# Attention and a spectral filter on one core: the first four scores ahead of the branch, three loads moved

## Chip, core and metric

The kernel runs on one core of a Trainium2 chip. The metric is the device time of one execution in microseconds, median of several runs. A profiled execution beside them gives the trace from which all rows below are taken.

## What is computed

Two independent blocks on inputs of 2048 rows by 448 columns, joined along the last axis:

```python
# A: 16 heads of 28, one common key and value (float32)
q = (x @ wq).reshape(B, S, H, Dh).transpose(0, 2, 1, 3)
k, v = x @ wk, x @ wv
p = softmax(einsum("bhqd,bkd->bhqk", q, k) * Dh ** -0.5)
a = einsum("bhqk,bkd->bhqd", p, v).transpose(0, 2, 1, 3).reshape(B, S, H * Dh) @ wo
# B: filter in the frequency domain
y = irfft2(rfft2(x) * (w_r + 1j * w_i), s=(S, D))
```

## The kernel before

**Stages.** A first stage projects x to q, k and v (L325), and interleaves with it the first transform of block B, in eight units q = 0 to 7: `fft1_a` (products L139, evicted to `a` at L145), then `fft1_b` (products L158, evicted to `bs` at L166 or L168 by `fft1_out`, and stored to `t1` in DRAM with two DMAs each, L173). Then comes a branch on the data, and behind it 256 steps of attention.

**The branch.** A shift for the softmax (`cvec`) is made from a bound. If the bound is too high (`bits` over a constant, L449), a loop computes exact maxima instead; with the inputs here the path is not taken. Every engine loads the value for itself (L448, TENSOR_LOAD), compares and branches. The branch cannot be interleaved with anything: what stands ahead of it in the program is issued ahead of it on its engine. The taken path writes two of the six PSUM banks `s0` to `s5`, and rebuilds the first q.

Just ahead of the branch stand: copies of the first q's high and low halves (`qh`, `ql`) into `qf`, done by ScalarE (L192), VectorE (L194), SP's and POOL's queues (L195); the products of unit 6 into two banks (`pb6`), the tiny products for `bits` (bank `pb3`, L434), unit 7's two halves (L139; the second one stays in bank `pa7`), and 16 transposes of v into a bank `pv` (L445). Right behind it stand the eviction of `pa7` (ScalarE, L145), those of `pb6` with its two stores, that of `pv` into `vs` (L486), and the second half of the keys `ka`: a cast (L254), a difference (L255) and three copies by SP (L257).

**The steps.** Step number `step` is one block of 128 keys for one group of four heads and 512 queries: four scores (L771, one bank each), four exponentials on ScalarE (L772) that free the banks, and later four products with `vs` (L747) into an output bank. Free banks are handed out by a queue (`take`, `scored`, `give`). PLAN is a list of batches of one to three steps; in a step's string each dash is a score and a letter is a unit of other work: F the last unit of the first transform (`fft1_b(7)`), A and B the halves of the second transform, W the output projection, Z the third transform. A batch's products with `vs` follow at its end. TensorE's order is that of the program; so is VectorE's behind the branch. The other queues are ordered by the library's planner, which places an instruction when its inputs are ready in its own estimate; `behind(x, y)` adds an order of issue and no wait.

**Loads for the transforms.** `at(step, f)` calls f at the end of a step. `fft2_load(0)` is called at step 0: four loads from `t1` by SP (L541) and four of the filter's weights by POOL (L546). They wait for the stores of unit 7. `fft2_split` (L558, L559) prepares the first A unit (L528). `build_q` for the second group stands at step 3: eight copies (L212) and one (L214) by SP.

After the last B unit, VectorE evicts it into `cst`, SP stores it to `t2` (L594), and `fft3_load(0)` reads it back as `c2` in four loads by SP (L609; r is the half, l the quarter in it), with the matrix `fi` loaded by POOL (L611). Their reader is `fft3_a` (L618).

Of the kernel before, what the change touches and what calls it, by code (L numbers as in the profile page):

```python
# [37 lines left out]
def batch(*units):  # L38

    return [("----" + u) if i else ("---" + u + "-") for i, u in enumerate(units)]  # L40


A, B, BACK = [batch(u, "", "") for u in "ABZ"]
CHUNK = 4 * [batch("W", "W", "W")] + 2 * [batch("W", "W", "")]
ONE, PAIR = batch(""), batch("", "")
PLAN = ([batch("F"), ONE] + 4 * [PAIR] + [batch("A", ""), A] + 10 * [B, A] + CHUNK + 4 * [B, A] + [B, B, ONE]
        + 5 * [BACK] + CHUNK + 14 * [BACK] + CHUNK + 13 * [BACK])

ROOM = {"A": 0, "B": 2, "W": 2, "Z": 1, "": 1, "F": 0}
# [7 lines left out]
def kernel(ctx: ExitStack, tc: tile.TileContext, t: dict):  # L57
    nc = tc.nc
    mm = nc.tensor.matmul
# [12 lines left out]
    ka = cp.tile([128, S], F32R, name="ka")  # L72
# [6 lines left out]
    def behind(ins, other):  # L79

        tc.add_manual_dep(ins.ins, other.ins.name,
                          mybir.DependencyInfo(mybir.DependencyClass.NoSync, mybir.DependencyReason.DATA),
                          reason="order of issue")
# [59 lines left out]
    def fft1_a_out(q, p, pa):  # L143
        a = at1[q, p] = fp.tile([128, 2, DF], F32, name="a", tag=("pwr", "pwi")[p])
        return nc.scalar.activation(a, pa, AF.Copy)  # L145
# [4 lines left out]
    def fft1_mm(q, pb=None):  # L150
        w = xb[q][1]
        if pb is None:
            pb = aux2("pbb"), ps_o.tile([128, 2, DF], F32, name="po")
        for p in range(2):
            a = at1.pop((q, p))
            for h in range(2):
                for e in range(2):
                    mm(pb[h][64 * e:64 * e + 64, p], w[64 * h:64 * h + 64, 2 * p + e], a[64 * h:64 * h + 64, e],  # L158
                       start=True, stop=True)
        return pb  # L160

    def fft1_out(q, pb, after=None):
        bs = fp.tile([128, 2, 2, DF], F32, name="bs", tag=("cst", "cst", "wr", "b2")[q // 2])
        for h in range(2):
            if q < 6:
                ev = nc.scalar.activation(bs[:, h], pb[h], AF.Copy)  # L166
            else:
                ev = nc.vector.tensor_copy(bs[:, h], pb[h])  # L168
                if after is not None:
                    behind(ev, after)  # L170
        for e in range(2):
            n0 = 16 * e + 2 * q
            stored.append(nc.sync.dma_start(t1.rearrange("(l s) n f -> s l n f", l=2)[:, :, n0:n0 + 2],  # L173
                                            bs[64 * e:64 * e + 64]))
        return ev
# [10 lines left out]
    qa = {}  # L186
# [35 lines left out]
    free = deque(ps_s.tile([128, 512], F32, name=f"s{i}") for i in range(BANKS))  # L222

    def bank():
        free.rotate(-1)
        return free[-1]

    def pair_of(b):
        return b[:, :2 * DF].rearrange("p (n f) -> p n f", n=2)


    with tc.tile_pool(name="w1", bufs=1) as w1:
# [37 lines left out]
        with tc.tile_pool(name="x1", bufs=2) as x1:  # L270
# [104 lines left out]
            for c in range(1, NC):  # L375
                for g in range(NG):
# [22 lines left out]
                    n = 4 * (c - 1) + g  # L399
                    if n in slots:  # L400
                        q = slots.index(n)
                        fft1_a(q)
                        fft1_load(q + 4)
                        if n == 10:
# [3 lines left out]
                            qf, qh, ql = build_q(0, 0, True)  # L408
# [22 lines left out]
        pb6 = fft1_mm(6, [pair_of(bank()) for _ in range(2)])  # L431
# [3 lines left out]
        bound = nc.vector.tensor_reduce(bits, pb3[0:1, 0:16], axis=AX.X, op=ALU.max)  # L435
# [7 lines left out]
        pv = bank().rearrange("p (b d) -> p b d", b=16)  # L443
        for b in range(16):
            nc.tensor.transpose(pv[:, b], kf[32:64, b * 128:(b + 1) * 128], ident[32:64, 32:64])  # L445


        rv = nc.values_load(bits.bitcast(I32)[0:1, 0:1])  # L448
        with tc.If(rv > int(np.float32(BOUND).view(np.int32))), tc.tile_pool(name="g1", bufs=1) as g1:  # L449
            k4 = g1.tile([128, S], F32, name="k4")  # L450
            nc.vector.memset(k4, 0.0)
            for i in range(4):
                nc.vector.tensor_copy(k4[32 * i:32 * i + DH], kf[0:DH])
            mz = g1.tile([128, 4, 32], F32, name="mz")
            nc.vector.memset(mz, 0.0)


            qv = qraw.rearrange("p g (b q) -> p (g b) q", q=128)
            banks = free[2], free[3]
            with tc.For_i(0, 64, 1) as n:  # L460
                qs = g1.tile([128, 128], F32, name="qs")
                nc.vector.tensor_copy(qs, qv[:, bass.ds(n, 1)][:, 0])
                mx = g1.tile([128, 4, 4], F32, name="mx")
                for i in range(4):
                    r = slice(32 * i, 32 * i + 32)
                    for h in range(4):
                        ps = banks[0]
                        mm(ps, qs[r], k4[r, h * 512:(h + 1) * 512], start=True, stop=True)
                        nc.vector.tensor_reduce(mx[:, i, h:h + 1], ps, axis=AX.X, op=ALU.max)
                nc.vector.tensor_reduce(mz[:, :, DH], mx, axis=AX.X, op=ALU.max)  # L470
                pt = banks[1][:, :128]
                mm(pt, mz.rearrange("p i d -> p (i d)"), ident, start=True, stop=True)
                nc.vector.scalar_tensor_tensor(qs, qs, mask, pt, op0=ALU.mult, op1=ALU.add)
                nc.vector.tensor_copy(qv[:, bass.ds(n, 1)][:, 0], qs)
            nc.vector.memset(cvec, 0.0)
            nc.vector.memset(mask, 1.0)
            qf, qh, ql = build_q(0, 0, True)
            for i in range(4):
                for p in range(4):
                    on_dve = copy_q(i, p, qf, (qh, ql)[p % 2], nc.vector)  # L480
            on_act = nc.scalar.activation(bits, bits, AF.Copy)


        behind(fft1_a_out(7, 1, pa7), on_act)
        on_dve = fft1_out(6, pb6, on_dve)
        ev = nc.vector.tensor_copy(vs, pv)  # L486
        behind(ev, on_dve)
        on_dve = ev
# [2 lines left out]

    ctx.enter_context(tc.manual_schedule(engines={mybir.EngineType.DVE}))

    d, f, a, b, e, c = free
    free.clear()
    free.extend((a, b, d, e, f, c))
    take, late = free.popleft, []

    def give(bank, scores=1):

        late.append([scores, bank])
# [10 lines left out]
    begun = []  # L512
# [88 lines left out]
    t2v = t2.rearrange("(r l n) h f -> r l h n f", r=2, l=2)  # L601
    c2 = {}

    def fft3_load(q):
        c2["c", q] = fp.tile([128, 4, DF], F32, name="c2", tag="b2")
        for r in range(2):
            for l in range(2):
                p = (r * 2 + l) * 32
                nc.sync.dma_start(c2["c", q][p:p + 32], t2v[r, l][:, 4 * q:4 * q + 4])  # L609
        c2["F", q] = fp.tile([128, 4, 128], F32, name="fi", tag="wr")  # L610
        behind(nc.gpsimd.dma_start(c2["F", q], t["fi"][:, 4 * q:4 * q + 4]), begun[-1])  # L611

# [80 lines left out]
    def at(step, f, *a):  # L693
        later.setdefault(max(step, 0), []).append((f, a))
# [8 lines left out]
    place, where, room = [], {}, []  # L703
    for b, steps in enumerate(PLAN):
        for i, s in enumerate(steps):
# [4 lines left out]
        first = units[:1] == "Z" and (len(where["Z"]) - 1) % 4 < 2  # L710
        room.append(2 if first else ROOM[units[:1]])
    fft2_consts()
    at(0, fft2_load, 0)
    at(where["A"][0] - 1, fft2_split, 0)
    at(14, fft3_consts)
    for u, step in enumerate(where["A"]):
# [10 lines left out]
    for g in range(NC * NG - 1):  # L727
        n = next(n for n in range(16 * g + 3, 16 * g + 13) if place[n][1] < 2 and room[place[n][0]])
# [10 lines left out]
    step = 0  # L739
# [19 lines left out]
    for c, g in order:  # L759
        for kc in range(16):  # L760
            ps, n = [], 0
            b, i = place[step]
            for k in PLAN[b][i]:
                if k != "-":
                    f, *a = todo[k].popleft()
                    f(*a)
                    continue
                if n % 2 == 0:
                    ps.append(pp.tile([128, 2, CW], F32, name="p"))
                sc = take()  # L770
                begun.append(mm(sc, ka[:, kc * 128:(kc + 1) * 128], qa[c, g][:, n], start=True, stop=True))  # L771
                nc.scalar.activation(ps[-1][:, n % 2], sc, AF.Exp, scale=SCALE)  # L772
                scored(sc)
                n += 1
            pend.append((c, g, kc, ps))
            if i + 1 == len(PLAN[b]) and step < 255:
                flush(min(KEEP, len(PLAN[b])))
            if step == 1:
                give(ps_x.tile([128, 512], F32, name="sx", tag="aux"))
                give(ps_o.tile([128, 512], F32, name="po"))  # L780
            for f, a in later.pop(step, []):
                f(*a)
            if step in builds:
                build_q(*order[step // 16 + 1])
            elif norms and i < 2 and room[b] and step > waits_for_output(norms[0][0]):
                room[b] -= 1
                norm(*norms.popleft())
            step += 1
# [3 lines left out]
    c = NC - 1  # L792
# [15 lines left out]
    for k in range(4):  # L808
        p = ws[k]
# [120 lines left out]
```

## Time and profile before

| | us |
|---|---|
| median of 3 runs | 657.26 (657.15 to 657.98) |
| profiled execution | 655.57 |
| its span | 653.8 |
| TensorE busy in the span | 646.0 |
| ScalarE busy | 554.9 |
| VectorE busy | 361.7 |

The profiled execution is one execution, 1.69 us under the median of the three runs; times inside it are counted from the start of the span. The granted clock was 1.00. Busy shares of TensorE overlap by modelled ends of pipelined products, so a share of 99% does not say that it runs at its peak; the wait lists and the times from one row to the next say more. In rows, "idle before <-x" names what ended the engine's idle time, as inferred from the semaphores.

### The profile page before, as it was taken

The page shows a single profiled execution, that of the slowest core. Times are in us where ns is not written, and L with a number is a line of the kernel's source. Part 1 is how long each engine was busy: PE and PEld are TensorE (multiplying, and loading weights), DVE is VectorE, ACT ScalarE, POOL GpSimd, SP SyncE. Part 2 cuts the span into 40 slices and gives each one's busy share as a digit, 9 for nine tenths or more (in the row PEclk, how much of TensorE's full clock was granted, in tenths as well). Part 3 has the DMA queues.
Part 4 walks back from the last instruction along what each step waited for, and adds up shares of the span by engine and source line. Part 5 has one row for each costly group of instructions (what it writes and reads, how often), then busy time and mean ns, then how long its engine had stood idle before and what let it go on. Part 6 is the DMA issues. An engine that isn't in the chain of part 4 may idle for free.

```text
span 653.8 us, 11925 instructions
## 1 busy us (share of the span) xinstructions
PE 646.0 (99%) x4480; PEld 377.3 (58%) x4480; DVE 361.7 (55%) x810; ACT 554.9 (85%) x1100; POOL 59.2 (9%) x109
## 2 busy tenths in 40 slices
PE   9999999999999999999999999999999999999997
PEld 6877554555545566455545655656565565565655
DVE  6999546767788832377763601465533421553533
ACT  5555899999999988899989987999999788999991
POOL 3022301101101100000000000010011000010010
PEclk9999999999999999999999999999999999999999
DMA  8756952525453323121151303123231403240001
GB/s 281 255 174 168 255 149 77 140 69 147 123 144 86 94 70 93 44 61 50 48 147 55 84 29 78 43 77 76 74 79 33 106 29 94 59 110 15 14 29 58
DMA packets 34572, 62.40 MB, mean 95 GB/s; under 512 B 6657, under 2 KB 22930, under 8 KB 33548
## 3 DMA queue, kind: packets, MB, share of 16 engines
q1 hardware_dynamic: 30736, 49.44, 26.8%
q0 software_dynamic: 3200, 11.26, 6.7%
q8 instruction: 36, 0.59, 0.4%
q10 hardware_dynamic: 576, 0.92, 0.4%
q14 instruction: 24, 0.20, 0.1%
HBM read 29.35 MB, written 14.75 MB: 67 GB/s over the span
## 4 chain that ended last, share of the span: by engine, by line
PE 86%; SPq 1%; DMA 1%; DVE 1%; ACT 0%; issue 0%; ACTq 0%; DVEq 0%
PE s L771 29%; PE s L747 28%; PE sx L771 5%; PE po L771 5%; PE po L747 4%; PE s L667 4%; PE sx L747 2%; PE s L630 2%; PE s L618 1%; PE sx L667 1%; PE po L667 1%; SPq L212 1%; PE s L530 1%; PE s L529 1%; PE s L528 1%; PE sx L618 1%
## 5 line engine op out<-in xcount | busy, mean ns | idle before, releaser
L772 ACT ACTIVATE p<-s 128x512 f32<-128x512 f32 x767 | 416.7, 651 | 48.3 <-PE s L771 48.0
L771 PE MATMUL s<-qa,ka 128*128 128x512 f32 x767 | 238.3, 408 | 1.0 <-DVE vs L486 1.0
L747 PE MATMUL s<-p,vs 128*32 128x512 f32 x1664 | 193.8, 596 | 0.0
L771 PEld LDWEIGHTS s<-qa,ka 128*128 128x128 f32 x767 | 138.7, 188 | 88.8 <-ACT p L772 50.7
L747 PEld LDWEIGHTS s<-p,vs 128*32 128x32 f32 x1664 | 46.8, 109 | 105.0 <-issue 100.5
L772 ACT ACTIVATE p<-sx 128x512 f32<-128x512 f32 x133 | 86.3, 649 | 2.5 <-PE sx L771 2.5
L772 ACT ACTIVATE p<-po 128x512 f32<-128x512 f32 x124 | 79.9, 644 | 2.8 <-PE po L771 2.8
L655 DVE RECIPROCAL r<-r 128x128 f32<-128x128 f32 x64 | 61.0, 953 | 2.2
L771 PE MATMUL sx<-qa,ka 128*128 128x512 f32 x133 | 53.1, 399 | 0.0
L771 PE MATMUL po<-qa,ka 128*128 128x512 f32 x124 | 50.3, 405 | 0.0
L638 POOL TENSOR_TENSOR yo<-y 128x226 f32<-128x226 f32 x16 | 10.1, 632 | 292.8 <-issue 252.7
L674 DVE COPY ya<-s 128x448 f32<-128x448 f32 x7 | 4.4, 625 | 56.8 <-PE s L667 56.8
L771 PEld LDWEIGHTS sx<-qa,ka 128*128 128x128 f32 x133 | 25.0, 188 | 10.8 <-ACT p L772 5.9
L747 PE MATMUL po<-p,vs 128*32 128x512 f32 x256 | 29.9, 596 | 0.0
L771 PEld LDWEIGHTS po<-qa,ka 128*128 128x128 f32 x124 | 23.3, 188 | 10.0 <-ACT p L772 6.2
L632 DVE COPY m<-s 128x452 f32<-128x452 f32 x13 | 8.2, 629 | 33.9 <-PE s L630 33.9
L620 DVE COPY z<-s 112x512 f32<-112x512 f32 (+1 forms) x11 | 7.6, 692 | 33.6 <-PE s L618 30.7
L325 PE MATMUL s<-xh,wqh 128*128 128x512 f32 x64 | 25.8, 403 | 0.2 <-ACT wqh L307 0.2
L325 PE MATMUL s<-xh,wql 128*128 128x512 f32 x64 | 25.1, 392 | 0.1
L329 ACT ACTIVATE qraw<-s 128x512 f32<-128x512 f32 x16 | 9.3, 600 | 16.7 <-PE s L325 16.6
L755 DVE COPY osb<-s 128x512 f32<-128x512 f32 x12 | 8.3, 690 | 21.5 <-PE s L747 21.5
L656 DVE TENSOR_TENSOR osb<-osb,r 128x128 f32<-128x128 f32 x64 | 18.7, 292 | 2.2
(188 smaller groups left out, 717.0 us busy)
## 6 DMA issues: line engine op xcount, KB each, us to landing
qa<-qa SPq DMA_DIRECT2D x15, 512.0 KB, 5.4
raw<-xa SPq DMA_DIRECT2D x16, 256.0 KB, 5.0
xb<-xb SPq DMA_DIRECT2D x8, 512.0 KB, 3.5
qa<-qh SPq DMA_DIRECT2D x64, 64.0 KB, 2.0
qa<-ql SPq DMA_DIRECT2D x60, 64.0 KB, 2.0
ob<-yo SPq DMA_DIRECT2D x16, 226.0 KB
t<-bs SPq DMA_DIRECT2D x16, 225.0 KB, 3.4
wr<-wr POOLq DMA_DIRECT2D x16, 225.0 KB, 4.2
```

The source lines that it names most:

```text
L325: mm(pq, w[:, j, gs], x[:, j], start=(j == 0 and n == 0), stop=(j == 3 and n == 1))
L329: out = nc.scalar.activation(qraw[:, g, cs], pq, AF.Copy)
L618: mm(pz[:w, j], c2["c", q][:, j, o0:o0 + w], c2["F", q][:, j], start=True, stop=True)
L630: mm(py[:, k], z[:w, r, js], cs3[:w, k], start=True, stop=True)
L638: nc.gpsimd.tensor_tensor(yo[:, 0:2], y1[:, 0], y1[:, 1], op=ALU.add)
L655: nc.vector.reciprocal(r, r)
L656: nc.vector.tensor_tensor(o, o, r, op=ALU.mult)
L667: mm(p, x[c][:, g, s], w[:, g], start=(g == 0 and n == 0), stop=(g == NG - 1 and n == 2))
L747: mm(po[c, g][32 * i:32 * i + 32], vs[:, kc], ps[i // 2][:, i % 2], start=(kc == 0), stop=(kc == 15))
L755: nc.vector.tensor_copy(o, po[c, g])
L771: begun.append(mm(sc, ka[:, kc * 128:(kc + 1) * 128], qa[c, g][:, n], start=True, stop=True))
L772: nc.scalar.activation(ps[-1][:, n % 2], sc, AF.Exp, scale=SCALE)
```

## The change

The first step's four scores are written once ahead of the branch (`first_scores`), into the banks `a`, `b`, `d`, `f`, and a second time at the end of the taken path, which overwrites their inputs. Step 0 no longer issues them; its exponentials read those banks. The queue of free banks starts with the two others. Unit 6's evictions (`fft1_out(6, ...)`), with their two stores, stand ahead of the branch, since they free `d` and `f`. In step 0 the unit F follows all four scores and no longer stands between the third and the fourth. The loop of the taken path uses the banks `a` and `b`, which are the same as before. `fft2_load(0)` is called at step 1, and two of the four `c2` loads of `fft3_load(0)` (r = 1) are issued by POOL.

```diff
-PLAN = ([batch("F"), ONE] + 4 * [PAIR] + ...
+PLAN = ([["----F"], ONE] + 4 * [PAIR] + ...
@@ ahead of the branch, behind the transposes
+        fft1_out(6, pb6, bound)
+
+        d, f, a, b, e, c = free
+        begin = a, b, d, f
+
+        def first_scores():
+            for n, s in enumerate(begin):
+                mm(s, ka[:, :128], qf[:, n], start=True, stop=True)
+
+        first_scores()
@@ in the taken path
-            banks = free[2], free[3]
+            banks = a, b
...
             on_act = nc.scalar.activation(bits, bits, AF.Copy)
+            first_scores()
@@ behind the branch
         behind(fft1_a_out(7, 1, pa7), on_act)
-        on_dve = fft1_out(6, pb6, on_dve)
...
-    d, f, a, b, e, c = free
     free.clear()
-    free.extend((a, b, d, e, f, c))
+    free.extend((e, c))
@@ fft3_load
-                nc.sync.dma_start(c2["c", q][p:p + 32], t2v[r, l][:, 4 * q:4 * q + 4])
+                eng = nc.gpsimd if q == 0 and r else nc.sync
+                eng.dma_start(c2["c", q][p:p + 32], t2v[r, l][:, 4 * q:4 * q + 4])
@@ the plan of loads
-    at(0, fft2_load, 0)
+    at(1, fft2_load, 0)
@@ the steps
-                sc = take()
-                begun.append(mm(sc, ka[:, kc * 128:(kc + 1) * 128], qa[c, g][:, n], start=True, stop=True))
+                if step:
+                    sc = take()
+                    begun.append(mm(sc, ka[:, kc * 128:(kc + 1) * 128], qa[c, g][:, n], start=True, stop=True))
+                else:
+                    sc = begin[n]
```

More of the change, by code (lines that the diff above doesn't have):

```diff
@@ L45 @@
 ONE, PAIR = batch(""), batch("", "")
-PLAN = ([batch("F"), ONE] + 4 * [PAIR] + [batch("A", ""), A] + 10 * [B, A] + CHUNK + 4 * [B, A] + [B, B, ONE]
+PLAN = ([["----F"], ONE] + 4 * [PAIR] + [batch("A", ""), A] + 10 * [B, A] + CHUNK + 4 * [B, A] + [B, B, ONE]
         + 5 * [BACK] + CHUNK + 14 * [BACK] + CHUNK + 13 * [BACK])
```

## The prediction

> **What bounds the kernel now.** I read the page first, then TensorE's waits, then the two places those waits name.
>
> ```profile
> span 653.8 us, 11925 instructions
> PE 86%; SPq 1%; DMA 1%; DVE 1%; ACT 0%; issue 0%; ACTq 0%; DVEq 0%
> PE s L771 <- DVE vs L486: 1.0, 1, 1.0
> PE sx L618 <- DMA c<-t: 0.9, 1, 0.9
> ```
>
> The first two lines are of the page (span, chain), the others of TensorE's waits. TensorE is the chain nearly from end to end, and inside the span it stands still visibly at only two places the change touches: 1.0 us ahead of the first score (L771) and 0.9 us ahead of the first product of the last transform (L618). So the change has about 1.9 us to win there, and everything else of it must be checked for harm.
>
> Windows after the first score show how a shift there is passed on:
>
> ```profile
> 73.00:82.00 9.00, 9.00 (x53) 3.98 (x51) 2.40 (x5) 8.89 (x19) 1.94 (x4) 1.00 1.00 303
> 82.00:94.50 12.50, 12.50 (x83) 6.09 (x75) 3.52 (x7) 12.50 (x28) 0.00 (x0) 1.00 0.61 157
> ```
>
> Columns: window, length, then PE, PEld, DVE, ACT, POOL busy, granted clock, DMA share, GB/s. ScalarE is busy 8.89 of 9.0 us and then 12.5 of 12.5 us: the exponentials run back to back, and TensorE, also full by its modelled ends, follows the banks they free. A shift of the row of exponentials is therefore a shift of everything behind it; later, when filter units join (L528), TensorE alone sets the pace and keeps the shift.
>
> **The branch, before.** The same moment on PE, on PE's sequencer (PEldq) and on ACT:
>
> ```profile
> 68.58 1.18 PE L445 MATMUL s<-ident,kf 32*128 32x32 f32 x16
> 70.78 0.94 PE L771 MATMUL s<-qa,ka 128*128 128x512 f32 x3 [1.01 <-DVE vs L486]
> 71.64 0.41 PE L158 MATMUL pbb<-a,fw 64*64 64x225 f32 x2
> 72.56 1.44 PE L771 MATMUL s<-qa,ka 128*128 128x512 f32 x5
> L448 PEldq TENSOR_LOAD <-bits x1: 755/755/755, 69.1 to 69.1; - x1
> L449 PEldq COMPARE_BRANCH  x1: 352/352/352, 70.0 to 70.0; - x1
> L449 PEldq EVENT_SEMAPHORE  x1: 51/51/51, 70.4 to 70.4; - x1
> L448 SPq TENSOR_LOAD <-bits x1: 1129/1129/1129, 68.6 to 68.6; - x1
> 71.34 1.58 ACT L772 ACTIVATE p<-s 128x512 f32<-128x512 f32 x3 [1.78 <-PE s L771]
> 73.11 5.50 ACT L772 ACTIVATE p<-s 128x512 f32<-128x512 f32 x11 [0.19 <-PE s L771]
> ```
>
> The transposes end at 69.76, but the load of the branch value, begun at 69.1, the compare and the event on the path not taken last until 70.45, and the first score stands at 70.78. That is 1.35 us of branch, and the wait "for vs" is a coincidence in time: the branch itself held TensorE. Exponentials stand (5.50-0.72)/10 = 0.478 us apart. The fourth came at 73.11 after a break of 0.19, so the unbroken row behind it is the one that a first exponential at 73.11-3x0.478 = 71.68 would have begun. 71.68 is the mark to beat.
>
> **Four scores ahead of the branch.** Nothing is computed more often on this path; four L771 are moved. Their inputs and banks:
>
> ```profile
> 67.31 0.85 DVE L194 CAST qa<-qh 32x512 fp32r<-32x512 f32 x2
> 68.64 1.16 DVE L168 COPY bs<-s 128x450 f32<-128x450 f32 x2 [0.48 <-DVEq L449]
> 69.80 0.69 DVE L486 COPY vs<-s 128x512 f32<-128x512 f32 x1
> 68.30 0.55 ACT L145 ACTIVATE a<-s 128x450 f32<-128x450 f32 x1
> 70.06 1.23 SPq L173 DMA_DIRECT2D t<-bs  x2
> 71.39 0.78 SPq L257 DMA_DIRECT2D ka<-ka  x1
> 64.89 1.51 POOL L195 DMA_DIRECT2D qa<-ql  x3
> DMA to landing us min/median/max: 3.2/3.8/4.1
> ```
>
> The last landing row belongs to L195. The last of POOL's three copies is issued at about 65.9 (64.89+2x0.5) and lands 3.8 (at most 4.1) later, at 69.7 (70.0). Banks: a is free after `bits`, b after the ACT copy at 68.85, d and f after the two small evictions, which now follow the casts at 68.16 without the 0.48 us of DVE's branch and end at 69.32. So the scores run right behind the transposes, 0.235 us apart ((1.44-0.50)/4): the fourth starts by 70.46 and ends by 70.96.
>
> Their exponentials cannot use that early start fully. The taken path writes the same four banks again, so the reader behind the join waits for a count that TensorE raises only at its event on the path not taken. TensorE's load began 0.66 us before the transposes had ended, so it waits for dispatch, not for completion; I put it at 69.75, when the last copy is in. 69.75+1.35 = 71.1 for the event, 71.2 for the first exponential. Gain against the mark: 0.5 us. Bounds: with a load at 69.4 the event still waits for the fourth score (70.96), gain 0.6; if the load waits for the end of the fourth score, the first exponential comes at 70.96+1.35+0.1 = 72.4, a loss of 0.7.
>
> Are scores five to eight in time? Filter's products (L158) follow the event by 0.3 as the first score did: 71.4; the next score stood 0.92 us behind their start (71.64 to 72.56): 72.3; its exponential 0.55 later (72.56 to 73.11): 72.87, while ScalarE is ready for it at 71.2+4x0.478 = 73.1. Covered by 0.24 us; the break of 0.19 goes.
>
> **The evictions and their stores ahead of the branch.** On DVE they cost nothing: 1.16 us that hide DVE's own load, and `vs` (L486) waits for the transposes (69.76) anyway. On SP the two stores (now at 70.06) start at 69.3 and end at 70.6, but its load of 1.129 us (now at 68.6) comes behind them, and 0.33 us later, as now from 69.73 to 70.06, the `ka` copies: 72.0 instead of 71.39. The two `kl` copies behind wait for DVE in any case, so the last store is 0.3 to 0.6 us later; I take 0.4.
>
> **The filter's first loads, one step later.** Their reader is the first L528:
>
> ```profile
> 84.84 1.78 SPq L541 DMA_DIRECT2D b<-t  x4
> 86.66 0.52 SPq L212 DMA_DIRECT2D qa<-ql  x1
> 89.13 0.59 SPq L212 DMA_DIRECT2D qa<-ql  x1
> 88.93 0.40 DVE L558 CAST bh<-b 128x450 fp32r<-128x450 f32 x1 [13.40 <-DMA b<-t]
> 89.36 0.63 DVE L559 TENSOR_TENSOR b<-b,bh 128x450 fp32r<-128x450 f32 x1
> 91.05 0.37 PE L528 MATMUL po<-bh,g1h 128*128 128x450 f32 x1
> ```
>
> The split is done at 89.99, TensorE wants it at 91.05-0.5 = 90.55: 0.56 us of cover, and the 0.4 of SP fit in. POOL has no other work there, so its four loads stay. Cost nothing; without the cover each further us of delay costs one.
>
> **Two of four c2 loads on POOL.** (Chain of waits, PE timeline, the rows of L611, then the landings of L611 and of L520.)
>
> ```profile
> 331.51 2.70 DMA t<-cst
> 334.23 0.33 SPq L609
> 334.60 1.38 SPq L609
> 336.03 0.45 SPq L609
> 336.52 3.02 DMA c<-t
> 339.68 1.10 PE L618 MATMUL sx<-fi,c 128*113 128x128 f32 x8 [0.91 <-DMA c<-t]
> L611 POOL DMA_DIRECT2D fi<-fi x8: 543/546/560, 294.7 to 582.2; - x8
> DMA to landing us min/median/max: 3.8/4.4/5.3
> DMA to landing us min/median/max: 2.8/3.1/4.2
> ```
>
> SP issues four loads one behind the other from 334.23; the last starts at 336.52 and lands at 339.54. With r=1 on POOL, SP's second, issued by 335.98, is in at 338.6 at the latest (the last one landed 3.02-0.43 = 2.6 behind the end of its issue); POOL's start at 334.3 and 334.3+0.54 = 334.8. Nearest rows for POOL's landing: 3.1 (L520, 128 rows) to 4.4 (L611), so 337.9 to 339.2. At the low end the whole 0.91 us goes, at the high end 0.34, at the longest row (5.3) a loss of 0.6. The loads are half the size of L611's; I take 3.6: 338.4, so that SP's second decides (338.6); the stall is gone but for crumbs: 0.85 us.
>
> [...]
>
> **Sum.** 0.5+0.85 = 1.35 us. The profiled execution took 655.57 (span 653.8), so 654.2; the median of the runs shown stands 1.69 higher, at 657.26, and I subtract there: 655.9. 0.2%, about what a measurement of this kernel can tell from no change, is 1.31 us: the forecast stands on that edge.
>
> **Rivals.**
> 1. *TensorE's load waits for the scores.* For it: it stands in the same queue, and the four carry more waits than the transposes. Against: in the row it began before the transposes had ended. Its price is -0.7 instead of +0.5; with the c2 part 657.1, no change. Chance 0.15.
> 2. *POOL is no faster,* or fi's load comes to stand behind the two waiting loads (issue at 335.4, landing 3.8 to 5.3 later: 339.2 to 340.7). For it: 4.4 median. Against: POOL issues its first fi at 294.7, 40 us ahead of the store that the c2 loads wait for. Then 0.5 us in all or less: 656.8. Chance 0.23.
> 3. *The filter's first loads come late: slower.* SP's order is the planner's. Five L212 of the next q stand behind the four L541 now, 0.63 apart (86.66 to 89.13). If the loads, made a step later, are put behind all of them, b comes up to 5x0.63 = 3.15 us later, with SP's 0.4 it is 3.55: the split ends at 93.5 and L528 stands there instead of at 91.05. That is 2.5 us against before, the 0.5 of the branch is lost in it, 0.85 is won back at c2: 658.9, slower by 1.65 us. It decides from a delay of 0.56 us on. Against: the q copies that do not wait for a queue's turn would slip into the 5 us in which SP now stands before L541. Chance 0.12.
>
> **How the numbers follow.** The forecast has 0.50, rivals 0.15, 0.23, 0.12. Over 0.2% faster needs both parts near full: most of the forecast's share, 0.44. Rivals 1 and 2 and the forecast's weaker part: same 0.45. Slower 0.11: rival 3 mostly, and rivals 1 and 2 at their bad ends together. Range: below, both caps and a little (0.6+1.0, and 0.2 for what only the queue orders decide): 655.2; above, into rival 3: 658.0.
>
> **What would show it.** Right: four L771 at 69.6 to 70.5 with no idle before them; PE's load near 69.8 and event near 71.1; the first L772 near 71.2, then none of the 0.19 us break; first L528 near 90.5 without wait; POOL rows of c2 at 334; L618's idle below 0.2. Wrong: an event on PE after 71.6, an L528 waiting for L559, or L618 still waiting 0.5 us for a POOL load or for fi.

## The result and the profile after

| | before | after |
|---|---|---|
| median of 22 runs each, taken together | 656.43 us | 658.53 us |
| profiled execution | 655.57 us | 657.95 us |
| its span | 653.8 us | 656.2 us |

The ratio is 1.0026, 95% interval 1.0014 to 1.0038: slower by 0.26%. The forecast was 655.9 us, 0.2% faster, with a range of 655.2 to 658.0: the sign was wrong, and the time lies above the range. The medians of before run from 656.27 to 657.42 from one set of runs to the next, so kernels below are compared by the ratio within their own set.

The lines after, as for before: page, TensorE's waits, and the two windows behind the first score.

```profile
span 656.2 us, 11931 instructions
PE 86%; DMA 1%; ACT 0%; DVE 0%; ACTq 0%; issue 0%; SPq 0%; DVEq 0%
PE sx L629 <- DMA c<-t: 3.0, 1, 3.0
PE pbb L158 <- PEq L459: 0.6, 1, 0.6
73.00:82.00 9.00, 9.00 (x52) 4.12 (x48) 3.01 (x6) 9.00 (x20) 2.46 (x5) 1.00 1.01 306
82.00:94.50 12.50, 12.50 (x79) 6.10 (x75) 2.82 (x6) 12.50 (x28) 0.00 (x0) 1.00 0.62 160
```

The wait ahead of the first score (1.0) has become one of 0.6 ahead of filter's products. The wait at the first products of the last transform, which was to vanish, went from 0.91 to 3.00 us (L618 is L629 here). The windows are as full as before.

**The branch.** One row fixes the clock times of the two traces against each other: the reduction to `bits`, of which nothing ahead was changed. It stands at 67.11 before and at 67.94 after; these 0.83 us are taken off below (in all fourteen profiles the row stands between 66.8 and 69.8). VectorE's, TensorE's and ScalarE's timelines and the branch's own rows:

```profile
67.11 0.16 DVE L435 TENSOR_REDUCE bits<-s 1x1 f32<-1x16 f32 x1
```

```profile
67.94 0.16 DVE L435 TENSOR_REDUCE bits<-s 1x1 f32<-1x16 f32 x1
69.41 1.18 PE L445 MATMUL s<-ident,kf 32*128 32x32 f32 x16
70.52 1.20 PE L453 MATMUL s<-qa,ka 128*128 128x512 f32 x4
72.34 0.41 PE L158 MATMUL pbb<-a,fw 64*64 64x225 f32 x2 [0.63 <-PEq L459]
L458 PEldq TENSOR_LOAD <-bits x1: 793/793/793, 70.9 to 70.9; - x1
L459 PEldq EVENT_SEMAPHORE  x1: 51/51/51, 72.2 to 72.2; - x1
72.37 2.07 ACT L786 ACTIVATE p<-s 128x512 f32<-128x512 f32 x4 [1.30 <-PEq L459]
```

The scores run right behind the transposes, and the first exponential stands at 72.37-0.83 = 71.54, 0.14 ahead of the mark of 71.68 instead of 0.5. TensorE's load began at 70.9, that is 70.1 in before's times, 0.35 later than forecast. The first filter product (L537) stands at 91.79, 90.96 in before's times (there 91.05), without a wait.

**The loads of c2.** Chain, TensorE's timeline, and the rows of L620 (c2) and L622 (fi):

```profile
332.31 2.69 DMA t<-cst
335.02 0.33 SPq L620
335.39 6.87 DMA c<-t
342.40 1.10 PE L629 MATMUL sx<-fi,c 128*113 128x128 f32 x8 [3.00 <-DMA c<-t]
L620 POOL DMA_DIRECT2D c<-t x2: 558/564/571, 335.7 to 336.3; - x2
L622 POOL DMA_DIRECT2D fi<-fi x1: 560/560/560, 336.8 to 336.8; - x1
c<-t SPq DMA_DIRECT2D x6, 112.5 KB, 6.2
c<-t POOLq DMA_DIRECT2D x2, 112.5 KB, 4.2
fi<-fi POOLq DMA_DIRECT2D x1, 256.0 KB, 6.5
```

The kernel before issues the same load of fi, its second, 15 us before c2's first load (334.23):

```profile
L611 POOL DMA_DIRECT2D fi<-fi x1: 543/543/543, 319.2 to 319.2; - x1
```

The last three rows of the view after are DMA issues from 333 to 345 us, with the median time to landing. What ends the stall is not a load on POOL. It is SP's second load, which left 335.39 and landed 6.87 later; before, SP's four took 3.0 to 3.7. POOL's own two landed at 339.72 and 340.70, while TensorE was ready at 342.40-3.00 = 339.40: even without SP's late load it would have waited 1.3 us. And POOL's queue has a third transfer: the fi of the next eight points, 256 KB, which had been loaded at 319 us and now stands behind the two waiting loads. A ring here is the packets of one issuer's queue. The packet records of the two rings in the kernel after, added up by the start of a packet for each half microsecond (KB; SP's packets of c2 are 900 B, POOL's 2700 to 4500 B):

```
from us     337.5  338.0  338.5  339.0  339.5  340.0  340.5  341.0  341.5  342.0
POOL ring      57     95     49     53    108     94     25      8      4      0
SP ring       114      2     37     60     38     39    106     91    106     57
```

Together the rings move about as much as SP's alone did before (124 KB per half microsecond from 337.5 to 340.5; before 115, 125, 90, 137, 126 from 336.5 on). In these 3 us POOL's ring moves 456 KB and SP's 289, in the half microsecond from 338.0 only 2. A load counts as landed with the last of sixteen completion counts in the trace. Of SP's second load ten had come by 340.26, the other six came from 340.60 to 342.26; before, its sixteen came within 0.36 us. So the stall is set by the slowest few parts of that load.

### The profile page after: what moved, and what is told of

The parts are those of the page before. It is cut to its first block, busy times and chain, and to the rows that moved or that the text cites. A ratio compares the mean times of both kernels' runs of the same rounds, so it can differ in the third digit from the quotient of the medians.

```text
span 656.2 us, 11931 instructions
## 1 busy us (share of the span) xinstructions
PE 646.9 (99%) x4480; PEld 377.9 (58%) x4480; DVE 361.3 (55%) x810; ACT 554.8 (85%) x1100; POOL 60.6 (9%) x111
## 4 chain that ended last, share of the span: by engine, by line
PE 86%; DMA 1%; ACT 0%; DVE 0%; ACTq 0%; issue 0%; SPq 0%; DVEq 0%
PE s L783 29%; PE s L758 28%; PE sx L783 5%; PE po L783 5%; PE po L758 4%; PE s L678 4%; PE sx L758 2%; PE s L641 2%; PE s L629 1%; PE sx L678 1%; DMA c<-t 1%; PE po L678 1%; PE s L539 1%; PE s L538 1%; PE s L537 1%; PE sx L629 1%
```

## Experiments

Each kernel was run 12 times beside runs of the kernel before on the same chip, unless it says one execution. "Stall" is TensorE's wait at fft3's first products in the profiled execution. "Low clock" counts runs whose mean granted TensorE clock was 0.997 or less, for a reason that the second experiment shows.

| kernel | ratio to before, 95% interval | stall, us | low clock |
|---|---|---|---|
| before (three sets, 87 runs) | 1 | 0.9; 0.6 | 42 of 87 |
| after (22 runs) | 1.0026 [1.0014, 1.0038] | 3.0; 2.4 | 17 of 22 |
| branch part alone | 0.9989 [0.9976, 1.0002] | 0.6 | 0 of 12 |
| c2 part alone | 1.0019 [1.0001, 1.0036] | 1.9 | 6 of 12 |
| after, fi ahead of c2 on POOL | 0.9993 [0.9977, 1.0009] | 1.7 | 2 of 12 |
| branch part, value load first | 0.9990 [0.9977, 1.0003] | 0.6 | 1 of 12 |
| before, scores issued twice | 1.0008 [0.9994, 1.0022] | 0.9 | 1 of 12 |
| branch part, q's build earlier | 0.9986 [0.9971, 1.0000] | 0 | 3 of 12 |
| the same again | 0.9982 [0.9964, 1.0000] | 0 | 3 of 12 |
| the same, value load first | 0.9986 [0.9971, 1.0002] | 0 | 2 of 12 |
| before, q's build earlier | 0.9990 [0.9973, 1.0007] | 0 | 4 of 12 |

### Either part alone

```diff
 # the branch part alone: the kernel after with
-                eng = nc.gpsimd if q == 0 and r else nc.sync
+                eng = nc.sync
```

> The kernel after, with all four loads of c2 back on SP (and so the second load of fi no longer behind waiting loads on POOL's queue); the start and the branch stay as changed. Theory: the whole loss is in the stall at fft3's first products, 3.00 us in the kernel after against 0.91 before. Then this stall comes back to 0.8 to 1.0 us, the last landing of c2 to about 3.6 us after SP's issues (before: 3.7 us), and the time is that of the kernel before less the branch part as the two traces show it, 0.1 to 0.2 us: ratio to before 0.9990 to 1.0000. Rival, by my forecast of the branch part: 0.5 us faster, ratio 0.9992. Rival, that the start or the branch carries part of the loss in a way that only shows later: ratio over 1.0010 with a stall under 1 us.

```diff
 # the c2 part alone: the kernel before with
-                nc.sync.dma_start(c2["c", q][p:p + 32], ...
+                eng = nc.gpsimd if q == 0 and r else nc.sync
+                eng.dma_start(c2["c", q][p:p + 32], ...
```

> The kernel before, with only the two r = 1 loads of c2's first eight points moved to POOL's queue. Theory: this edit alone makes the loss: SP's second load again lands last, 6 to 7 us after its issue, the stall at fft3's first products is 2.7 to 3.2 us against 0.91, ratio to before 1.0028 to 1.0036 (1.8 to 2.3 us). Rival, that the loss needs the other edits too (another order of banks and units, the start): the stall stays under 1.5 us, ratio under 1.0012.

The TensorE rows of the two, branch part first:

```profile
340.12 1.10 PE L629 MATMUL sx<-fi,c 128*113 128x128 f32 x8 [0.59 <-DMA c<-t]
```

```profile
342.49 1.10 PE L619 MATMUL sx<-fi,c 128*113 128x128 f32 x8 [1.86 <-DMA c<-t]
335.93 6.43 DMA c<-t
```

The loss is in the c2 part: alone it is slower (1.0019, lower bound only 1.0001; I had expected 1.0028 to 1.0036), and without it the kernel is not (0.9989). Its stall of 1.86 lies between my two expectations, not at 2.7 to 3.2, though SP's second load again lands last, 6.43 after it left. In identical code the stall differs from execution to execution (3.00 and 2.39 in two profiles of the kernel after, 0.91 and 0.63 in two of the kernel before), so the stall of a single profile is good to half a microsecond or so. The 0.59 of the branch part alone, expected at 0.8 to 1.0, is no less than before's second.

### A second look at the kernel after: the clock

Most runs of the kernel after show a granted clock of 0.994 to 0.997, the profiled one 0.999. The c2 part's profile had shown what such a run looks like, there at the branch. Windows of 1 us; the third column from the right is the granted clock:

```profile
71.28 0.93 PE L772 MATMUL s<-qa,ka 128*128 128x512 f32 x3 [0.97 <-DVE vs L486]
71.00:72.00 1.00, 0.72 (x3) 0.50 (x3) 0.93 (x3) 0.15 (x1) 0.86 (x2) 1.00 0.96 174
72.00:73.00 1.00, 1.00 (x13) 0.60 (x16) 1.00 (x1) 1.00 (x3) 0.28 (x1) 0.57 0.80 167
73.00:74.00 1.00, 1.00 (x13) 0.35 (x5) 0.05 (x1) 0.42 (x1) 1.00 (x3) 0.50 0.79 254
74.00:75.00 1.00, 1.00 (x3) 0.81 (x4) 1.00 (x2) 0.33 (x1) 0.76 (x2) 0.50 0.93 333
75.00:76.00 1.00, 1.00 (x8) 0.54 (x6) 0.96 (x3) 1.00 (x3) 0.55 (x1) 0.72 1.12 418
```

> The kernel after once more, for a second profile. Of its 22 runs 17 show a granted clock of 0.994 to 0.997 (mean 659.1 us), 5 one of 0.999 (mean 656.8 us, the profiled one among them). In the profile of the c2 part alone the whole loss of clock lies in one place: 0.50 to 0.57 from 72 to 75 us, right behind 1.0 us in which TensorE stood idle at the branch. Theory: the changed kernel fills that gap and loses the clock at another place, right behind the 3 us stall at fft3's first products, where a half clock of some 3.3 us costs 1.6 us more. Then a profile of clock 0.997 shows 0.5 in the 4 us behind the stall (about 342 to 346) and 1.0 at 72 to 76. Rival: it loses it at the branch as before, 0.5 at 72 to 76 and 1.0 behind the stall.

One execution, clock 0.996:

```profile
341.23 2.02 PE L629 MATMUL sx<-fi,c 128*113 128x128 f32 x8 [2.39 <-DMA c<-t]
340.00:341.00 1.00, 0.00 (x0) 0.00 (x0) 0.00 (x0) 0.05 (x1) 0.00 (x0) 1.00 1.11 223
341.00:342.00 1.00, 0.77 (x4) 0.80 (x5) 0.00 (x0) 0.00 (x0) 0.00 (x0) 0.55 0.77 157
342.00:343.00 1.00, 1.00 (x7) 1.00 (x6) 0.00 (x0) 0.00 (x0) 0.00 (x0) 0.50 0.02 3
343.00:344.00 1.00, 1.00 (x5) 0.81 (x4) 0.64 (x3) 0.29 (x1) 0.00 (x0) 0.50 0.00 0
344.00:345.00 1.00, 1.00 (x5) 0.82 (x4) 0.97 (x3) 1.00 (x3) 0.00 (x0) 0.74 0.02 8
```

The theory holds for this execution: at 72 to 76 us the clock is full, and right behind the stall it is half for (0.45+0.5+0.5+0.26)/0.5 = 3.4 us, the eight products taking 2.02 instead of 1.10 us. 3.4 us at half speed are 1.7 us of work, and that is what a low clock costs in the runs: in the three sets of before, the runs with 0.997 or less average 658.05, 657.46 and 657.38, the others 656.41, 655.78 and 655.66.

So the stall can have a second cost, the clock behind it (half for 3.4 us here, full in the first profile of this kernel, behind 3.00 us), and what the branch part gains, if it gains (its interval reaches 1.0002), is to lose the clock less often. By the runs, low clock is 42 of 87 in before, and 9 of 60 in the five sets with the branch part and all of c2 on SP (1 of 24 in the first two, 8 of 36 in the three below with q's build earlier). Why it is rarer is not shown: TensorE still idles at the branch, 0.2 to 1.4 us in the profiles with the changed start, 1.00 in the branch part alone against 1.01 before. The runs of the branch part alone, all with a full clock, average 656.32, those of before with a full clock, in the same set, 656.41: there is no gain to see.

A second profile of the kernel before, to catch the place of its low clock, did not catch one: one execution, clock 1.000 throughout.

> The kernel before once more, for a second profile. Of its 87 runs beside the last kernels 42 show a granted clock of 0.996 or 0.997. Theory: in such a run the clock is half for some 3.4 us right behind the idle microsecond at the branch, 72 to 76 us, as in the profile of the c2 part alone, and the span is 1.5 to 2 us longer; in the others it is 1.0 throughout, as in the first profile. So a clock of 0.997 goes with 0.5 at 72 to 76 us, a clock of 1.000 with none. Rival: a profile of 0.997 loses it elsewhere, at the first products of fft3 or in the first 20 us.

That before loses it at the branch is so inferred, from the c2 part's profile (same code up to 334 us) and from the counts; the last section shows a profile that loses it in the first 12 us.

### Which of POOL's transfers holds SP's load

```diff
 # fi ahead: the kernel after, in fft3_load
+        fis = []
+        for k in ((0, 1) if q == 0 else (q,) if q > 1 else ()):
+            c2["F", k] = fp.tile([128, 4, 128], F32, name="fi", tag="wr")
+            fis.append(nc.gpsimd.dma_start(c2["F", k], t["fi"][:, 4 * k:4 * k + 4]))
+            behind(fis[-1], begun[-1])
 ...
+                ld = eng.dma_start(c2["c", q][p:p + 32], ...
+                if q == 0 and r:
+                    behind(ld, fis[-1])
```

> The kernel after, with the second load of fi (256 KB) issued on POOL's queue ahead of the two loads of c2, as it comes in the kernel before (there at 319 us), instead of behind them (336.84 us in the kernel after). Theory 1, the shoved load of fi fills the DMA engines while SP's second load of c2 drains: the stall falls from 3.00 us to 1.2 or less, SP's second load lands within 4.5 us of its issue, ratio to before within 0.9985 to 1.0010. [...] Theory 3, that POOL's queue simply starts later (its issues come 0.7 us after SP's): the last landing would be one of POOL's own loads, the stall 1.5 to 2 us.

```diff
 # fi alone: the branch part alone, in fft3_load
 ...
+        fi = nc.gpsimd.dma_start(c2["F", q], t["fi"][:, 4 * q:4 * q + 4])
+        behind(fi, begun[-1])
+        if q == 1:
+            behind(fi, small[-1])
+        if q == 0:
+            tiny = fp.tile([32, 2, 4], F32, name="tiny", bufs=1)
+            for l in range(2):
+                small.append(nc.gpsimd.dma_start(tiny[:, l:l + 1], t2v[1, l][:, 3:4, :4]))
+                behind(small[-1], fi)
```

> The branch part alone (all of c2 on SP), with the second load of fi (256 KB) on POOL held behind two loads of 512 B that wait for the last store of t2, as it is held in the kernel after behind the two waiting loads of c2. So POOL carries fi at the same time as SP carries c2, and nothing of c2. Theory 1, that POOL's ring pushes SP's packets aside whatever it carries: the stall grows from 0.6 us to 1.5 us or more, and SP's last load of the first eight points lands 1 us or more later against its issue than in the branch part alone (3.2 us). Theory 2, that only the split of c2 itself matters: the stall stays under 1.0 us.

TensorE's rows, first with fi ahead, then with fi alone on POOL (one execution, clock 0.997), with the issues of the second from 333 to 346 us and its clock:

```profile
339.61 1.10 PE L634 MATMUL sx<-fi,c 128*113 128x128 f32 x8 [1.70 <-DMA c<-t]
```

```profile
342.16 1.31 PE L638 MATMUL sx<-fi,c 128*113 128x128 f32 x8 [2.72 <-DMA c<-t]
c<-t SPq DMA_DIRECT2D x8, 112.5 KB, 5.3
fi<-fi POOLq DMA_DIRECT2D x1, 256.0 KB, 5.0
343.00:344.00 1.00, 1.00 (x5) 0.90 (x4) 0.42 (x1) 0.07 (x1) 0.00 (x0) 0.50 0.00 0
345.00:346.00 1.00, 1.00 (x4) 0.81 (x3) 0.93 (x3) 1.00 (x4) 0.00 (x0) 0.50 0.00 0
```

With nothing of c2 on POOL, fi alone at the same moment makes a stall of 2.72 us and the half clock behind it: theory 1 of that run holds in this execution. With fi out of the way, the two loads of c2 alone still leave 1.70, over the 1.2 of theory 1 and within the 1.5 to 2 of theory 3, but not by the cause that theory 3 gives: again SP's second load lands last, not one of POOL's (SP's second 339.48, POOL's 338.14 and 339.03). So either lengthens the stall, whatever POOL's ring carries (2.72 and 1.70 us; 0.59 in the branch part alone). What share each had in the 3.00 us is not settled by single profiles; 1.70 in one and 1.86 in another with fi behind are too near each other for that.

The time of the runs says more. With fi ahead, and c2 still split, the ratio is 0.9993, where theory 1 put it (0.9985 to 1.0010), and the low clock falls from 17 of 22 to 2 of 12. That is 0.33%, or 2.2 us, under the kernel after: 0.7 to 1.3 from the stalls (2.39 and 3.00 less 1.70) and (17/22-2/12) x 1.7 = 1.0 from the clock. So the split of c2 alone costs no time that 12 runs can show (0.9993 beside 0.9989 for the branch part alone); the loss goes with fi pushed behind it.

Why a few parts of SP's load come so late beside POOL's packets (six of its sixteen counts from 340.60 to 342.26 in the kernel after), no run here shows.

### Scores as filling, and the value load

```diff
 # scores twice: the kernel before, ahead of the branch
+        for n in range(4):
+            mm(free[2 + n % 2], ka[:, :128], qf[:, n], start=True, stop=True)
```

> The kernel before, with the first step's four scores issued once more ahead of the branch, as mere filling: the step still does its own behind the branch. Nothing can start earlier by it. Theory, that the gain of the branch part is in the clock (half of the runs of the kernel before show 0.997, 658.05 us on average, the others 0.999 to 1.0 and 656.4): the runs with 0.997 fall from half to at most 3 in 12, ratio to before 0.9982 to 0.9994. Rival, that it comes from the scores standing ready when the branch ends: no gain here, ratio 0.9995 to 1.0010, and the clock of 0.997 still in about half of the runs.

Half of each: the low clock fell to 1 of 12 (10 of 23 beside it), as the clock theory said, but the ratio is 1.0008, where the rival put it. The runs with a full clock average 656.80 against 655.78 for before: 1.0 us lost for which I found no place (from `bits` to the end, the profile takes 586.71 us, before's two 586.67 and 585.95). That filling the gap keeps the clock is what the counts point to; that it pays by itself is not shown.

```diff
 # value load first: the branch part alone
         pv = bank().rearrange("p (b d) -> p b d", b=16)
+        rv = nc.values_load(bits.bitcast(I32)[0:1, 0:1])
         for b in range(16):
...
         first_scores()
-        rv = nc.values_load(bits.bitcast(I32)[0:1, 0:1])
```

> The first of these four kernels (branch part alone), with the branch's value load placed ahead of the 16 transposes, so that TensorE's sequencer reads the value some 1.5 us earlier. Theory 1, what set the branch's end in the kernel after is the moment at which TensorE's sequencer reaches its load (70.93 us), held by the event for the last copies of qf (70.74): the event can't come before those copies have landed, so the load moves ahead of it only if that event belongs to the scores; then the last engine to the branch's event is another and the first exponential comes 0.2 to 0.5 us earlier against the bits reduction than 4.43 us, ratio to the first kernel 0.9992 to 0.9997. Theory 2, the scores themselves, which need the copies, set the first exponential: no change, 4.3 to 4.5 us after the bits reduction, ratio 0.9998 to 1.0003.

No gain: 0.9990 beside 0.9989, and a first exponential at 4.36 us behind `bits`, where theory 2 put it. (Without the move it stands at 3.96 to 5.19, mean 4.56, in the seven profiles below, so one profile decides little.) Here another engine's load is last; the first exponential stands 0.66 behind SP's:

```profile
L443 PEldq TENSOR_LOAD <-bits x1: 558/558/558, 67.8 to 67.8; - x1
L443 SPq TENSOR_LOAD <-bits x1: 931/931/931, 69.7 to 69.7; - x1
71.31 3.05 ACT L786 ACTIVATE p<-s 128x512 f32<-128x512 f32 x6 [1.44 <-PEq L459]
```

Seven profiles with the changed start and TensorE's load behind the scores show what sets the first exponential there: it stands 0.64 to 0.66 us (once 0.78) behind the end of that load, which takes 0.49 to 1.46 us. (In three of the seven SP's load ends within 0.01 us of it, so there either may be the cause; in the other four SP's ends 0.04 to 0.49 after the exponential has begun.) One of the shortest and the longest (fi ahead; q's build earlier, again):

```profile
L458 PEldq TENSOR_LOAD <-bits x1: 495/495/495, 69.7 to 69.7; - x1
70.87 3.54 ACT L791 ACTIVATE p<-s 128x512 f32<-128x512 f32 x7 [0.89 <-PEq L459]
```

```profile
L458 PEldq TENSOR_LOAD <-bits x1: 1456/1456/1456, 71.2 to 71.2; - x1
73.30 1.08 ACT L786 ACTIVATE p<-s 128x512 f32<-128x512 f32 x2 [2.04 <-PEq L459]
```

Against `bits` the fourth exponential comes at 5.40 to 6.63, mean 6.00, in these seven, and at 5.73 to 6.24, mean 5.97, in four profiles with the old order behind the branch and a full clock there (one of them with the scores issued twice; 5.88 without it). On average the branch part moves nothing.

### The copy ahead of c2 in SP's queue, and a better kernel

```diff
 # q's build earlier: in the plan of the steps
-        n = next(n for n in range(16 * g + 3, 16 * g + 13) if ...
+        n = 112 if g == 7 else next(n for n in range(16 * g + 3, 16 * g + 13) if ...
```

> The branch part alone (all of c2 on SP), with the build of group 8's q moved from step 117 to step 112, so that its 512 KB copy no longer stands in SP's queue ahead of the loads of c2. Theory, that in the branch part alone the remaining stall of 0.6 us at fft3's first products is the wait for that copy to drain (8192 B packets until 337.5 us in the kernel after): the stall falls under 0.2 us, ratio to before 0.9978 to 0.9988, 0.6 us under the branch part alone. Rival, that the moved build's vector work or its copies come in the way of an A or B unit 5 steps earlier: a new stall of 0.5 us or more between 290 and 325 us, no gain over the branch part alone.

> All of c2 on SP, the branch part, the build moved to step 112, and TensorE's value load ahead of the transposes: the candidate for a version faster than both kernels. From the runs so far: the stall at fft3's first products gone (0.9 us of the kernel before), the granted clock of 0.997 in at most 3 of 12 runs instead of about half (0.8 us on average), 0.1 to 0.3 us at the branch: ratio to before 0.9968 to 0.9985. If the value load's place counts for nothing it equals the next kernel.

> The same without the value load's move, a second set of runs beside the last one's 0.9986 [0.9971, 1.0000]: expected 0.9972 to 0.9988.

> The kernel before with only the build of group 8's q moved from step 117 to step 112, nothing of the change. Theory, that the stall of 0.91 us in the kernel before is the wait for that copy, and that the clock is lost at the branch whatever happens here: the stall falls under 0.2 us, ratio 0.9984 to 0.9992, and the granted clock of 0.997 or less still in about half of the runs, at 72 to 76 us where the profile catches it. Rival, that the clock is lost behind this stall of 0.91 us in the kernel before: the runs with 0.997 fall to 3 in 12 or fewer and the ratio to 0.9980 or less.

TensorE's row of the first of these (L629 follows the scores at once) and the issues from 333 to 346 us:

```profile
341.68 1.04 PE L629 MATMUL sx<-fi,c 128*113 128x128 f32 x8
c<-t SPq DMA_DIRECT2D x8, 112.5 KB, 2.6
```

The stall is gone in all four; the old 0.91 us was the wait for the 512 KB copy that SP had queued ahead, and no other issuer was needed to remove it. Build and branch part together give 0.9986 and 0.9982, both intervals ending at 1.0000: 0.14 to 0.18% under before, which 12 runs do not quite show, and by the quotient of the ratios 0.4% under the kernel after. Both lie where they were expected. The value load's place adds nothing: 0.9986, just outside the 0.9968 to 0.9985 expected. The build alone gives 0.9990, as expected, with an interval that takes in 1; its low clock, 4 of 12, decides neither theory.

## Why the prediction was wrong, step by step

- **c2, forecast +0.85 us, the step that failed.** Two assumptions carried it. SP's second load was put at 338.6 "at the latest", 4.0 us behind its issue at 334.60: it left as forecast (335.39 less the 0.80 by which the store came later here), but the rate was shared with POOL's transfers (289 KB of SP's ring beside 456 of POOL's from 337.5 to 340.5), and it landed 6.87 after. I priced POOL's landing by its own rows, never SP's landing with POOL beside it. POOL's rows did not hold either: its loads left 0.7 behind SP's first instead of 0.1, landed 4.0 and 4.4 behind their issue instead of 3.6, and the second stood at 340.70-0.80 = 339.9 instead of 338.4. And of POOL's queue I looked at the first fi only (issued at 294.7, "40 us ahead"); the second, at 319 before, is the one that went behind the waiting loads, and alone it makes a stall of 2.72. Rival 2 named this order, but priced it as fi's own late landing. No rival had SP's load as the victim. Instead of a gain of 0.85, the profile shows a loss of 2.09. A slower kernel had a chance of 0.11, for another cause (rival 3), and the range ended at 658.0, under that rival's own price of 658.9.
- **The lower end of the range** counts a cap of 1.0 us for this part. No run shows this cap: the stall of before is 0.91 us, none is left where the copy ahead of c2 comes earlier (four profiles), and with two loads on POOL it was 3.00 and 2.39.
- **The branch, forecast +0.5, bounds +0.6 and -0.7.** Mechanism right: path, event, exponential follow each other as worked out (load to exponential 1.44 us, forecast 1.45), and the break of 0.19 is gone. Mis-sized were the load's start, 70.1 instead of 69.75, and its duration, taken as one number of one execution (0.755) where it spreads from 0.49 to 1.46. The term is 0.14 in the profile shown, and 0.0 over seven. The sum also started from 657.26, a median of three runs; over 22 the kernel before takes 656.43.
- **Rival 1** does not hold: the load began at 70.93, before the last score had ended (70.52+1.20 = 71.72).
- **Rival 3 and the cover of filter's loads.** L567 split at 88.64, 87.81 in before's times (there 88.93): not later but earlier, no wait. Right that it costs nothing, but not for the reason given, a cover of 0.56 us against a delay of 0.4: there was no delay.
- **What no term held: the clock.** It was 1.00 in the profile of before, and so left out. In 42 of the 87 runs of before it is 0.997 or less, and in each of the four profiles of this case that show such a clock it is half for 3.4 us at one place; the change made that rarer ahead of c2, by the counts of the branch part, and brought it back behind the longer stall, where one profile shows it. An estimate from these: stall +1.5 to +2.4 (2.39 and 3.00 less 0.91 or 0.63), low clock (17/22-42/87) x 1.7 = +0.5, branch 0.0 to -0.1: +1.9 to +2.9 us. The ratio's interval is 0.9 to 2.5 us. The stalls of the two profiles may not be typical: the five runs of the kernel after with a full clock average 656.84, only 0.4 to 1.2 over such runs of before in the three sets.

## What to carry to other kernels

Before a load goes to a second issuer, list what that issuer has queued behind it, and ask whose packets it will run beside: here the two rings together moved 124 KB per half microsecond, about what SP's alone had moved (90 to 137), and the load left on the first queue can become the last to land (6.87 us here instead of 3.0 to 3.7). If a load waits in a queue, look first for what stands ahead of it that could be moved earlier. And price a stall of TensorE with the clock behind it: one profile with a full clock does not say that most runs have it (here 17 of 22 had 0.997 or less).

## Not expected of the hardware

- The clock was half for 3.4 us behind idle times of 0.97, 1.50, 2.39 and 2.72 us of TensorE, and stayed full behind others of 0.6 to 3.00. The one of 1.50 us, in the first profile with q's build earlier, lies in the first 12 us, ahead of anything changed (one execution, clock 0.997):

```profile
7.48 0.69 PE L325 MATMUL s<-xh,wqh 128*128 128x512 f32 x1 [1.50 <-ACT wqh L307]
8.00:9.00 1.00, 1.00 (x3) 0.83 (x3) 0.97 (x3) 0.00 (x0) 0.00 (x0) 0.50 1.04 170
10.00:11.00 1.00, 1.00 (x4) 0.81 (x3) 0.54 (x1) 0.43 (x1) 0.00 (x0) 0.50 1.03 381
11.00:12.00 1.00, 1.00 (x5) 0.82 (x5) 0.97 (x3) 0.64 (x1) 0.18 (x1) 0.99 0.99 363
```

- By the windows of 1 us each of these half stretches is 3.4 us long (1.70 to 1.71 us of clock lost, at a half). They begin 1.8, 1.6, 2.3 and 3.5 us behind the start of the gaps of 0.97, 1.50, 2.39 and 2.72. Why the gap of 3.00 in the first profile of the kernel after did not cost the clock, and why about 1.0 us did in the c2 part's profile and not in that of the kernel before, is not shown.
- TensorE's load of one register from memory took from 0.49 to 1.46 us at the same place of the same code.
